# Inverse intermediate in contiguous weights, a second load of x, and a new order in a spectral filter and expert layer

## The chip, the core and the metric

The kernel runs on one core of a Trainium2 chip. The metric is the device time of one execution in microseconds (us), the median of three runs. Every instruction of the schedule is recorded first and issued later from one line, so the profile shows nearly all of them under line 552 (559 after the change), and they are told apart by the names of their tiles.

## What is computed

The input x has 2048 rows of 576 columns. It is normalised row by row, and two branches of the result are added to x. The reference, cut to what matters:

```python
xn = _layernorm(x, axis=-1)
# A: a filter in the two-dimensional spectrum
X = rfft2(xn)                      # 2048 x 289
y = irfft2(X * (w_r + 1j * w_i), (2048, 576))
# B: 32 heads, each picks one of 8 x 8 experts
q = einsum("nd,dhc->nhc", xn, w_q) # 32 heads, two halves of 128
s1, s2 = q1 . k1, q2 . k2          # 8 scores each
e = argmax(s1) * 8 + argmax(s2)
out = sum over heads of gelu(xn . u[e]) * v[e]
return x + y + out
```

The softmax over one candidate is 1.

## The kernel before

All Fourier transforms are matmuls with constant matrices. A row number is n = 16*n1 + t: n1 (128 values) lies on the partitions, t (16 values) counts tiles, so `XN` holds x as 16 tiles of 128 x 576. The stages, by the names in the program and the lines where they stand:

- `ln` (693), `folds` (733) and `dft128` (749), for each tile t: normalise, fold the 576 columns by symmetry to two parts of 289 (tiles `t`, `A`), and transform over n1 by matmuls. ScalarE or VectorE copies the results from PSUM (`banks`) to `AB`, four chunks of 128 partitions with 2048 columns, and `ABL`, the 66 rows left over. Columns are ordered in 16 groups of 128.
- `d_fwd` (990), two column groups at a time: the cosine and sine transform over the 576 columns. Its weights are 128 neighbouring columns of `AB` or `ABL` and its moving operand the constants `c` (145 columns). In fp32 each matmul is two weight loads and two matmul instructions in the profile. Result: `A2`, also named `A`.
- `s_fwd` (1016), four groups at a time with 32x32 weights `fw`, then `s_mul` (1032): the rest of the row transform, and the product with the filter `Wt` on VectorE (products into `y` and `t`, then two sums).
- `s_inv` (1044), two groups at a time: the first part of the inverse row transform. Its weights are columns of `y` (32 rows, tile position by row), its moving operand the 64 columns of `iv`. The 289 columns of `y` are covered by three chunks of 128 that start at 0, 161 and 49; the third is only there for the columns 128 to 160, and half of it is thrown away. The results are copied back over `AB` and `ABL`, to the same columns, one copy of 512 elements and two small ones for each group.
- `d_inv` (1067), for two tiles t and t+1: the inverse column transform, of the same shape as `d_fwd`. Row n of tile t stands in column 16*n + t of `AB`, so its weights are 128 columns that lie 16 elements (64 bytes) apart. Then ScalarE, VectorE and GpSimd unfold the result (`es` and `eo`, named `y` and `t` in the profile; the sum is named `A`).
- `fin` (1096), for each tile: the last 128-point transform and the experts' output are summed in PSUM, VectorE adds x from `XN` in place (`sc` is a scale), and SyncE stores the tile.
- The expert branch: `fold_part` (825) folds keys into `w_q` (32 loads `w` of 576 KB), `fold_scale`, `fold_end` and `fold_last` make the score weights `MU` and `MUL`; `x_t` (889) loads and scales x transposed (`xf`, `xT`); `scores` (905), `route` (932) and `combine` (954) compute, for two tiles, 448 scores and 64 expert activations, the maxima (`mx`), and the expert coefficients `CAT`. `wt`, `iv` and `id16` in these stages are small constants of their own.

The order is not that of the program. A planner (`_Plan`, 316) records every instruction with a modelled cost, groups matmuls, and then issues them by a list of priorities, `RANK` (142), under limits on PSUM tiles (`LIMIT`, 199). For work that several engines can do, `PICK` (133) holds one letter each: v VectorE, a ScalarE, g GpSimd. Each engine runs its instructions in order, and all DMAs are issued in order by SyncE.

Of the kernel before, what the change touches and what calls it, by code (L numbers as in the profile page):

```python
# [10 lines left out]
F32 = mybir.dt.float32  # L11
# [15 lines left out]
def _consts():  # L27
# [12 lines left out]
    k1 = np.arange(128) ^ np.arange(128) // 8 % 4 * 2  # L40
# [48 lines left out]
    iv = iv.reshape(8, 2, 128, 96).transpose(0, 2, 1, 3).astype(np.float32)  # L89
# [44 lines left out]
    "vgvgagvvvvaavggvgaavggvvaagggvaavgvvvaaavgvgvaavgvvavavvvgvavvggvvaavggvvvavvvvaavgvvvavagvvvgavgggv"  # L134
    "vavvvggaaaaagavggaggvvggavvgavggavavvgvggvggvaaaavvvvgvgavvagvaaavvvgagggavggagvaaavggvgvgggvaaaaaga"
    "gggavvgggvavvavvgavgggvggagaavaavgggggvgaavaavgaavgvavgggvavvvaavgavggavgggaavvavgggggggavvaaavvgvva"
    "aaaagvvvavagggggvgavggggagagvggvagagvgvgvvagggggagavvgvvagvvvgvgavagvgvg"
# [178 lines left out]
class _Plan:  # L316
# [9 lines left out]
    def cost(self, eng, m, out, ins, kw):  # L326
        n = 1
# [5 lines left out]
        if eng == "tensor":  # L333
# [3 lines left out]
            if kw.get("tile_position"):  # L337
                q = _parts(ins[0])
                return c * q[0] * q[1] / 16384, 230.0
# [873 lines left out]
```

## Time and profile before

| | |
|---|---|
| three runs | 253.95, 254.94, 255.24 us; median 254.94 |
| the profiled execution | 254.09 us, of which the span from the first to the last instruction is 252.3 |
| TensorE matmuls (PE) and weight loads (PEld) | 225.0 us busy (89%), 159.1 us (63%) |
| VectorE (DVE) | 195.0 us (77%) |
| ScalarE (ACT) | 76.2 us (30%) |
| GpSimd (POOL) | 107.7 us (43%) |
| moved by DMA | 41.75 MB, mean 165 GB/s |
| mean granted TensorE clock | 0.966 of full speed |

A row of a timeline gives the start, the length, the engine, the operation with output<-inputs, and in brackets the idle time before it with what ended it. A merged row's length reaches from the first start to the last end; TensorE's instructions overlap, so the distance of the starts tells the pace. A group's row gives the count, then the busy time, the mean ns of one, and the idle time just before.

### The profile page before, as it was taken

Reading aid. Unit: us, or ns where it says so; the run is one execution under the profiler, and the core shown is the slowest. Engines: PE = TensorE matmul, PEld = TensorE weight load, DVE = VectorE, ACT = ScalarE, POOL = GpSimd, SP = SyncE. Lnnn points to the kernel's source line nnn. Section 1 sums busy time; section 2 is a strip of 40 time slices with the busy share of each in tenths; the row PEclk is TensorE's granted clock in tenths of the full one; section 3 lists DMA queues with packets and bytes.
Section 4 is the critical chain, followed back from the end, with each engine's and each line's share of the span. In section 5 each row is a group of like instructions: output and inputs, shape, how many; then the busy total and the mean of one; then the engine's idle time right before and its main releaser. Section 6 shows DMA issues by size and latency. Waiting matters only on the chain.

```text
span 252.3 us, 6579 instructions
## 1 busy us (share of the span) xinstructions
PE 225.0 (89%) x2714; PEld 159.1 (63%) x2714; DVE 195.0 (77%) x458; ACT 76.2 (30%) x170; POOL 107.7 (43%) x155
## 2 busy tenths in 40 slices
PE   0335999999997898979999999989999999999994
PEld 0223756687466856875666444637788578888962
DVE  1979899946497168447977999998999897759574
ACT  2175853316304111372442320144220301110110
POOL 4557364523452006400650659364472464352330
PEclk9985899999999599999999999999999999999999
DMA  6999499999999649311231131013001111122116
GB/s 180 406 418 408 122 352 354 376 352 339 329 348 359 228 118 343 145 31 55 86 93 40 55 104 24 32 55 104 2 0 51 47 44 48 52 94 85 60 49 231
DMA packets 13998, 41.75 MB, mean 165 GB/s; under 512 B 1808, under 2 KB 4112, under 8 KB 13584
## 3 DMA queue, kind: packets, MB, share of 16 engines
q1 hardware_dynamic: 13968, 41.33, 46.3%
q8 instruction: 21, 0.34, 0.6%
q14 instruction: 9, 0.07, 0.1%
HBM read 36.61 MB, written 4.72 MB: 164 GB/s over the span
## 4 chain that ended last, share of the span: by engine, by line
PE 72%; DVE 15%; DMA 7%; issue 2%; ACT 1%; SPq 0%; POOL 0%; DVEq 0%; ACTq 0%
PE banks L552 72%; DMA w<-in_wq_dram 6%; DVE y L552 3%; DVE MT L552 2%; DVE w L552 2%; DVE t L552 2%; DMA c<-in_c_dram 2%; DVE A L552 1%; ACT AB L552 1%; DVE ABL L552 1%; DVE xT L552 1%; DVE mx L552 1%; DVE rr L552 0%; DVE xf L552 0%; SPq L552 0%
## 5 line engine op out<-in xcount | busy, mean ns | idle before, releaser
L552 PE MATMUL banks<-c,AB 128*128 128x145 f32 x256 | 50.1, 344 | 0.2 <-DVE ABL L552 0.2
L552 PEld LDWEIGHTS banks<-c,AB 128*128 128x128 f32 x256 | 46.8, 256 | 3.9 <-issue 1.4
L552 PE MATMUL banks<-MU,xT 128*128 128x512 f16 x192 | 45.9, 379 | 0.0
L552 PE MATMUL banks<-act,A 128*32 128x128 f32 (+1 forms) x256 | 27.5, 315 | 18.3 <-DVE act L552 10.5
L552 PEld LDWEIGHTS banks<-act,A 128*32 128x32 f32 (+1 forms) x256 | 21.4, 167 | 25.6 <-DVE act L552 10.5
L552 PEld LDWEIGHTS <-xT 128*128 128x128 f16 x224 | 20.8, 98 | 25.2 <-issue 1.9
L552 POOL TENSOR_TENSOR xT<-xf,xT 128x512 f16<-128x512 f32 (+1 forms) x23 | 20.4, 891 | 35.1 <-DVE xT L552 27.2
L552 POOL TENSOR_TENSOR y<-y,t 128x289 f32<-128x289 f32 x24 | 18.8, 810 | 30.0 <-DVE t L552 25.7
L552 POOL TENSOR_TENSOR A<-t 128x287 f32<-128x287 f32 (+3 forms) x32 | 23.1, 734 | 15.9 <-DVE t L552 7.3
L552 PEld LDWEIGHTS banks<-iv,y 32*128 32x128 f32 x768 | 23.6, 196 | 5.5 <-issue 2.5
L552 PE MATMUL banks<-iv,y 32*128 32x64 f32 x768 | 24.6, 282 | 2.6 <-issue 2.0
L552 PE MATMUL banks<-A,c 128*128 128x288 f32 x64 | 21.4, 416 | 0.0
L552 ACT ACTIVATE y<-banks 128x580 f32<-128x580 f32 x13 | 8.0, 651 | 42.0 <-PE banks L552 34.0
L552 ACT ACTIVATE AB<-banks 128x512 f32<-128x512 f32 x24 | 14.7, 616 | 18.8 <-PE banks L552 17.7
L552 PE MATMUL banks<-w,KP 128*32 128x288 f32 x256 | 20.2, 416 | 0.0
L552 POOL TENSOR_TENSOR t<-y 128x288 f32<-128x288 f32 x10 | 6.9, 692 | 22.0 <-ACT y L552 20.2
L552 POOL TENSOR_TENSOR t<-XN 128x289 f32<-128x289 f32 x15 | 12.5, 842 | 7.3 <-DVE A L552 3.1
L552 PE MATMUL banks<-c,ABL 32*128 32x145 f32 (+2 forms) x256 | 15.6, 357 | 0.0
L552 PE MATMUL banks<-A,fw 32*32 32x289 f32 x512 | 14.7, 413 | 0.2 <-ACT ABL L552 0.2
L552 DVE TENSOR_TENSOR A<-t 128x288 f32<-128x288 f32 (+3 forms) x32 | 14.6, 467 | 0.2
L552 DVE COPY ABL<-banks 64x128 f32<-64x128 f32 (+1 forms) x18 | 5.0, 288 | 12.2 <-ACT AB L552 9.0
L552 DVE SCALAR_TENSOR_TENSOR XN<-banks,sc,XN 128x576 f32<-128x576 f32 (+1 forms) x18 | 13.2, 746 | 1.3 <-PE banks L552 1.2
(130 smaller groups left out, 350.3 us busy)
## 6 DMA issues: line engine op xcount, KB each, us to landing
w<-in_wq_dram SPq DMA_DIRECT2D x32, 576.0 KB, 5.4
xf<-in_xT_dram SPq DMA_DIRECT2D x16, 320.0 KB, 3.0
Wt<-in_W_dram SPq DMA_DIRECT2D x8, 578.0 KB, 6.4
out_dram<-XN SPq DMA_DIRECT2D x14, 288.0 KB, 2.1
XN<-in_x_dram SPq DMA_DIRECT2D x3, 1154.0 KB, 10.2
XN<-in_x_dram SPq DMA_DIRECT2D x2, 577.0 KB, 5.2
iv<-in_iv_dram SPq DMA_DIRECT2D x8, 96.0 KB, 3.4
fw<-in_fw_dram SPq DMA_DIRECT2D x4, 192.0 KB, 6.2
```

Source lines behind the costliest of these rows:

```text
L552: fn(*[x.place() if isinstance(x, _Ps) else x for x in args], **{k: x.place() if isinstance(x, _Ps) else x for k, x in kw.items()})
```

## The change

1. `s_inv` writes to a new place and in a new layout. `XN` becomes a view of a larger tile `XI`, and after the folds are done the inverse intermediate lies in the same memory: for each tile t, four chunks of 128 neighbouring columns (`YT`) and one of the rest (`YLT`). `d_inv` takes these as weights. To make the layout one with matmuls that write 64 neighbouring columns, the constants `iv` are reordered: the moving operand is now 16 pieces of four elements, six apart. A copy from PSUM now writes single elements, 64 elements apart at the innermost step and 512 between tiles, and the copy of 512 elements is split in two of 256.
2. The third chunk of `s_inv` covers the 48 columns from 113 on, and its results take 48 partitions. In `d_inv` the leftover weights have 32 or 16 rows instead of 32.
3. x is overwritten by that, so `load_x` fetches it again, 16 loads of 288 KB into the memory of `AB`, which `d_fwd` has read by then. 14 tiles fit; the last two are loaded over the first two when these have been stored. `fin` adds from there.
4. The constants `wt`, `iv` (of the scores) and `id16` move into memory that the folds of `w_q` use, and so are written after these instead of early. The scratch of `ln` on ScalarE moves to a tile with six buffers. `iv` of `s_inv` has two buffers, not three.
5. The planner's cost of a matmul counts the weight load too, and `PICK` and `RANK` are new throughout.

```diff
-    k1 = np.arange(128) ^ np.arange(128) // 8 % 4 * 2
+    k1 = np.array([8 * g + 2 * (a ^ g % 4) + e for e in range(2) for a in range(4) for g in range(16)])
...
-    iv = iv.reshape(8, 2, 128, 96).transpose(0, 2, 1, 3).astype(np.float32)
+    iv = iv.reshape(16, 128, 3, 2, 16).transpose(0, 1, 4, 2, 3).reshape(8, 2, 128, 96).transpose(0, 2, 1, 3).astype(np.float32)
...
-    "vgvgagvvvvaavggvgaavggvvaagggvaavgvvvaaavgvgvaavgvvavavvvgvavvggvvaavggvvvavvvvaavgvvvavagvvvgavgggv"
+    "gggvavvvvaaavvvvavagvgggavggvvaaagvgvvvavgvvvvvvgggvavgvvvaaavgvgaaavvvgvaavgvvvaaggvgvavgvvgaaavvvg"
...
-    256, 294, 356, 417, 432, 525, 87, 484, 865, 888, 985, 269, 467, 374, 627, 757, 101, 541, 404, 387, 622,
+    239, 247, 252, 274, 291, 333, 222, 276, 218, 144, 412, 349, 225, 369, 299, 318, 473, 216, 99, 226, 109,
...
-    XN = K([128, 16, D + 1], F32, "XN")
+    XI = K([128, 10240], F32, "XI")
+    XN = XI[:, :9232].rearrange("p (t d) -> p t d", t=16)
+    YI = XI[:, :8192].rearrange("p (t c e k g) -> p c g k t e", t=16, c=2, e=4, k=4)
+    YL = XI[:, 8192:].rearrange("p (t e k g) -> p g k t e", t=16, e=2, k=4)
+    YT = XI[:, :8192].rearrange("p (t c n) -> p t c n", t=16, c=4)
+    YLT = XI[:, 8192:].rearrange("p (t n) -> p t n", t=16)
...
-                j, b = T([128, D], BF, "wa", 1, "t2"), rr[:, 3, t + i:t + i + 1]
+                j, b = T([128, D], BF, "wa", 6, "y"), rr[:, 3, t + i:t + i + 1]
...
-                        o = (0, 161, 49)[c]
-                        P.matmul(p[:, k, q, c, :], y[r, ri, o:o + 128], s[r, q, 32 * ri:32 * ri + 64],
+                        o, n = ((0, 128), (161, 128), (113, 48))[c]
+                        P.matmul(p[:n, k, q, c, :].rearrange("p (t e) -> p t e", e=4), y[r, ri, o:o + n],
+                                 s[r, q].rearrange("p (t e) -> p t e", e=6)[:, :, 2 * ri:2 * ri + 4],
                                  start=(ri == 0), stop=(ri == 1), tile_position=(32 * k, 0))
         for q in range(NQ):
-            pq = p[:, :, q]
-            FP.copy(ABg[:, :, g + q, :].rearrange("p c (k n) -> p c k n", k=4),
-                    pq[:, :, 0:2].rearrange("p k c (b n) -> p (c b) k n", b=2))
+            pq = p[:, :, q].rearrange("p k c (t e) -> p k c t e", e=4)
+            for c in range(2):
+                FP.copy(YI[:, c, g + q], pq[:, :, c])
             for b in range(2):
-                FP.copy(ABLg[64 * b:64 * b + 64, g + q, :].rearrange("p (k n) -> p k n", k=4),
-                        pq[64:128, :, 2, 32 * b:32 * b + 32])
+                FP.copy(YL[64 * b:64 * b + 48, g + q], pq[:48, :, 2, :, 2 * b:2 * b + 2])
...
-                    P.matmul(pv[b][:, c, q, :], ABt[:, 2 * (c ^ b) + b, :, t + q], ic[:, b, c ^ b, :], start=(q == 0), stop=False)
+                    P.matmul(pv[b][:, c, q, :], YT[:, t + q, 2 * (c ^ b) + b, :], ic[:, b, c ^ b, :], start=(q == 0), stop=False)
...
-                    r = slice(32 * i, 32 * i + 32)
-                    P.matmul(pv[b][:, c, q, :], ABLt[r, :, t + q], il[r, :], start=False, stop=(q == 1),
+                    r = slice(32 * i, 32 * i + 32 - i % 2 * 16)
+                    P.matmul(pv[b][:, c, q, :], YLT[r, t + q, :], il[r, :], start=False, stop=(q == 1),
                              tile_position=(32 * i, 0))
...
+    def load_x(t):
+        XR[t] = ABf[:, 576 * (t % 14):576 * (t % 14) + 576]
+        Q.dma_start(XR[t], xs[:, t, :D])
...
-        x = XN[:, t]
+        x = XR[t]
...
+    for t in range(14):
+        load_x(t)
     y = d_inv(0)
     for t in range(0, 16, 2):
         n = d_inv(t + 2) if t < 14 else None
         for q in range(2):
             fin(t + q, y[:, q])
+            if t + q < 2:
+                load_x(t + q + 14)
```

The new order shows in three places that the prediction uses.

On TensorE late in the program, before (`c_72,AB` and `c_72,ABL` are the large and small matmuls of `d_inv`, `A_93,c_68` the first of `fin`, `id_98,MT` transposes of coefficients, which read `banks<-MT` after the change):

```order
L552 MATMUL banks<-c_72,AB 128x145 x6
L552 LDWEIGHTS MT
L552 MATMUL banks<-id_98,MT 128x128
L552 LDWEIGHTS MT
L552 MATMUL banks<-id_98,MT 128x128
L552 MATMUL banks<-c_72,AB 128x145 x2
L552 MATMUL banks<-c_72,ABL 128x145 x8
L552 MATMUL banks<-A_93,c_68 128x288
```

And now:

```order
L559 MATMUL banks<-c_72,XI 128x145 x6
L559 LDWEIGHTS MT
L559 MATMUL banks<-MT 128x128
L559 LDWEIGHTS MT
L559 MATMUL banks<-MT 128x128
L559 MATMUL banks<-c_72,XI 128x145 x26
L559 MATMUL banks<-A_93,c_68 128x288
```

The weights of both kinds come from `XI` (x26 is the rest of one call of `d_inv` and a whole one behind it), and the matmuls stand between the same neighbours as before, the transposes and `fin`.

On VectorE, from the last copies of the score weights to the first maximum (`mx`), before:

```order
L552 SCALAR_TENSOR_TENSOR MU<-banks,sc,MU 128x4x112
L552 CAST xT<-xf 128x640
L552 SCALAR_TENSOR_TENSOR MUL<-banks,sc,MUL 64x336
L552 COPY A_93<-banks 128x2x2x145
L552 TENSOR_TENSOR xT<-xf,xT 128x512
L552 TENSOR_TENSOR y<-banks,Wt 128x578 x4
L552 TENSOR_TENSOR t_92<-banks,Wt 128x578 x4
L552 TENSOR_TENSOR y<-y,t_92 128x289 x2
L552 TENSOR_TENSOR xT<-xf,xT 128x512
L552 TENSOR_TENSOR xT<-xf,xT 64x128
L552 COPY A_93<-banks 128x2x2x145
L552 TENSOR_REDUCE mx<-banks 128x128
```

And now:

```order
L559 SCALAR_TENSOR_TENSOR MU<-banks,sc,MU 128x4x112
L559 COPY XI<-banks 48x4x32 x4
L559 COPY XI<-banks 128x4x16x4 x2
L559 TENSOR_SCALAR xf<-xf,bx 128x640
L559 COPY XI<-banks 48x4x32
L559 TENSOR_TENSOR xT<-xf,xT 64x128
L559 CAST xT<-xf 128x640
L559 TENSOR_REDUCE mx<-banks 128x128
L559 TENSOR_TENSOR t_92<-banks,Wt 128x578
```

Eight products of a group stood ahead of the maximum; now evacuations of `s_inv` (`XI<-banks`) stand there, and the four `t` products of a group follow the maximum.

On SyncE, from the middle of the weight loads to the last of them, before:

```order
L552 DMA w<-in_wq_dram 128x1152
L552 DMA fw<-in_fw_dram 128x384
L552 DMA Wt<-in_W_dram 128x1156 x2
L552 DMA w<-in_wq_dram 128x1152 x2
L552 DMA iv<-in_iv_dram 128x192
L552 DMA w<-in_wq_dram 128x1152 x2
L552 DMA iv<-in_iv_dram 128x192 x2
L552 DMA xf<-in_xT_dram 128x640 x2
L552 DMA w<-in_wq_dram 128x1152 x2
L552 DMA fw<-in_fw_dram 128x384
L552 DMA w<-in_wq_dram 128x1152
```

And now (`AB<-in_x` is the second load of x):

```order
L559 DMA w<-in_wq_dram 128x1152 x5
L559 DMA AB<-in_x_dram 128x576
L559 DMA xf<-in_xT_dram 128x640
L559 DMA AB<-in_x_dram 128x576
L559 DMA w<-in_wq_dram 128x1152 x3
L559 DMA Wt<-in_W_dram 128x1156 x2
L559 DMA w<-in_wq_dram 128x1152 x5
L559 DMA iv<-in_iv_dram 128x192
L559 DMA AB<-in_x_dram 128x576
L559 DMA Wt<-in_W_dram 128x1156
L559 DMA fw<-in_fw_dram 128x384
L559 DMA w<-in_wq_dram 128x1152 x3
```

Three of the second loads stand ahead of the last three weight loads; 13 come later.

More of the change, by code (lines that the diff above doesn't have):

```diff
@@ L133 @@
 PICK = (
-    "vgvgagvvvvaavggvgaavggvvaagggvaavgvvvaaavgvgvaavgvvavavvvgvavvggvvaavggvvvavvvvaavgvvvavagvvvgavgggv"
-    "vavvvggaaaaagavggaggvvggavvgavggavavvgvggvggvaaaavvvvgvgavvagvaaavvvgagggavggagvaaavggvgvgggvaaaaaga"
-    "gggavvgggvavvavvgavgggvggagaavaavgggggvgaavaavgaavgvavgggvavvvaavgavggavgggaavvavgggggggavvaaavvgvva"
-    "aaaagvvvavagggggvgavggggagagvggvagagvgvgvvagggggagavvgvvagvvvgvgavagvgvg"
+    "gggvavvvvaaavvvvavagvgggavggvvaaagvgvvvavgvvvvvvgggvavgvvvaaavgvgaaavvvgvaavgvvvaaggvgvavgvvgaaavvvg"
+    "aavgvvvvvvaavvgaavvgavvvvggvvagvvvvaggvgvvgvavvvaavvgaaggaavgavavavvvvvavvvggvvgggvaavavgggvvgvgaaav"
+    "vvvvvaagggaggvvaaavaaavavaagggaggvgaavaaggvggggvaaaaaaavvaaggaaggggavaaaaaaagaaggavgvvgaavaagggggggg"
+    "aaaavaaagavaavavavaaggvvvvavgvggavavgvvgagagvgggagagvvggagagggvgagaggvgvagavggggavvgvvgg"
 )
@@ L142 @@
 RANK = (
[55 rows of a table removed]
[58 rows of a table added]
 )
 LIMIT = {"x": 2, "a": 4, "b": 4, "q": 8, "c": 4, "s": 2, "f": 1, "m": 2}
-WORDS = {"st": 48, "t1": 578, "t2": 288, "A2": 580, "y": 580, "w": 1152, "Wt": 1156, "xf": 640, "xT": 576,
+WORDS = {"st": 48, "t1": 578, "A2": 580, "y": 580, "w": 1152, "Wt": 1156, "xf": 640, "xT": 576,
          "act": 128, "mx": 128, "fw": 384, "iv": 192}
 def _masks():
-    m = np.zeros((128, 99), np.float32)
+    m = np.zeros((128, 79), np.float32)
     code = 2.0 ** np.array([0, -6, -12, -18, -30, -36, -42, -48])
-    m[:, 20:27] = code[1:]
-    m[:, 27:35] = code
-    m[:, 35:99] = np.tile(2.0 ** np.array([-18, -12, -6, 0]), 16)
+    m[:, 0:7] = code[1:]
+    m[:, 7:15] = code
+    m[:, 15:79] = np.tile(2.0 ** np.array([-18, -12, -6, 0]), 16)
     return m
@@ L335, in cost @@
                 return max(n, 128) / 2.4 * (2 if ins[0].dtype == F32 else 1) + 4, 230.0
-            c = max(n, 64) / 2.4 + (2.5 if n > 256 else 5) if ins[0].dtype != F32 else max(n, 64) * 4 / 2.4 + 8
+            k = ins[0].shape[1]
+            if ins[0].dtype == F32:
+                c = 2 * max(n / 1.2 + 2, k * (1.7 if ins[0].ap[1][0] > 4 else 0.87))
+            else:
+                c = max(max(n, 64) / 2.4 + (2.5 if n > 256 else 5), 56 if k == 128 else k / 1.2)
             if kw.get("tile_position"):
                 q = _parts(ins[0])
-                return c * q[0] * q[1] / 16384, 230.0
+                c = max(c * q[0] * q[1] / 16384, 33.3 if ins[0].dtype == F32 else 16.6)
             return c, 230.0
@@ L618, in _body @@
     Q.dma_start(kT, a["kT"])
-    mk = K([128, 99], F32, "mk")
+    mk = K([128, 79], F32, "mk")
     Q.dma_start(mk, a["mk"])
-    cst = mk[:, 35:99]
+    cst = mk[:, 15:79]
     fm = K([128, 4], I32, "fm")
@@ L639, in _body @@
     ABL = K([128, S], F32, "ABL")
-    ABg = AB.rearrange("p c (g n) -> p c g n", g=16)
-    ABLg = ABL.rearrange("p (g n) -> p g n", g=16)
-    ABt = AB.rearrange("p c (n t) -> p c n t", t=16)
-    ABLt = ABL.rearrange("p (n t) -> p n t", t=16)
+    ABf = AB.rearrange("p c n -> p (c n)")
     MU = K([128, 2, 4, 512], F16, "MU")
@@ L983, in load_iv @@
     def load_iv(g):
-        IV[g] = T([128, 2, 96], F32, "iv", 3)
+        IV[g] = T([128, 2, 96], F32, "iv", 2)
         Q.dma_start(IV[g], a["iv"][g // 2])
@@ L1093, in d_inv @@
         return y
+    XR = {}
+    @staged
+    def load_x(t):
+        XR[t] = ABf[:, 576 * (t % 14):576 * (t % 14) + 576]
+        Q.dma_start(XR[t], xs[:, t, :D])
     @staged
@@ L1121, in _body @@
     plan.gate = gate
-    wt = K([128, 448], BF, "wt")
-    V.tensor_copy(wt.rearrange("p (e m) -> p e m", e=7), mk[:, 20:27].unsqueeze(2).to_broadcast([128, 7, 64]))
-    iv = K([128, 8, 32], BF, "iv")
-    V.tensor_copy(iv, mk[:, 27:35].unsqueeze(2).to_broadcast([128, 8, 32]))
-    id16 = K([128, 128], F16, "id16")
-    V.tensor_copy(id16, idn)
     plan.gate = set()
@@ L1139, in _body @@
                 fold_end(c)
+    wt = view(RM[:, 608:], [128, 448], BF)
+    V.tensor_copy(wt.rearrange("p (e m) -> p e m", e=7), mk[:, 0:7].unsqueeze(2).to_broadcast([128, 7, 64]))
+    iv = view(RM[:, 832:], [128, 8, 32], BF)
+    V.tensor_copy(iv, mk[:, 7:15].unsqueeze(2).to_broadcast([128, 8, 32]))
+    id16 = view(RM[:, 960:], [128, 128], F16)
+    V.tensor_copy(id16, idn)
     plan.gate = set(gate)
```

111 rows, old and new, of the table RANK are left out of this document.

## The prediction

> **What bounds the kernel now.** I read the page's 40 slices first, then the chain of work that ended last, then the engines' busy time by stretches. From the page, the span, the slices (tenths busy) of TensorE (PE) and VectorE (DVE), TensorE's granted clock, and what the DMA engines moved:
>
> ```profile
> span 252.3 us, 6579 instructions
> ...
> PE   0335999999997898979999999989999999999994
> ...
> DVE  1979899946497168447977999998999897759574
> ...
> PEclk9985899999999599999999999999999999999999
> ...
> GB/s 180 406 418 408 122 352 354 376 352 339 329 348 359 228 118 343 145 31 55 86 93 40 55 104 24 32 55 104 2 0 51 47 44 48 52 94 85 60 49 231
> ```
>
> A slice is 6.3 us. TensorE is at 9 in nearly every slice from the fifth on, and the DMA engines carry 329 to 376 GB/s from the sixth to the thirteenth, some 82 us, and little after 100. VectorE is at 8 or 9 over much of the second half, and mostly lower in the last seven slices. The end of the chain (start, us, what):
>
> ```profile
> 165.60 83.43 PE banks L552 x577
> 249.05 0.52 DVE XN L552
> ```
>
> So the last 83 us are TensorE's work end to end, without a wait. The first score matmul and the first maximum over scores on VectorE, from the timelines:
>
> ```profile
> 115.12 1.04 PE L552 MATMUL banks<-MU,xT 128*128 128x512 f16 x4
> ...
> 128.02 1.08 DVE L552 TENSOR_REDUCE mx<-banks 128x128 f32<-128x896 f32 x1
> ```
>
> Busy time by stretches cut there (PE, PEld, DVE, ACT, POOL, clock, DMA share, GB/s):
>
> ```profile
> 115.12:128.02 12.90, 12.90 (x216) 7.38 (x213) 11.03 (x17) 4.36 (x6) 5.76 (x8) 1.00 0.25 73
> 128.02:165.60 37.58, 36.51 (x515) 20.02 (x511) 33.87 (x73) 11.19 (x26) 18.54 (x25) 1.00 0.21 57
> 165.60:220.00 54.40, 54.40 (x400) 40.46 (x400) 48.63 (x105) 12.52 (x28) 27.27 (x36) 1.00 0.14 46
> 220.00:249.55 29.55, 29.01 (x179) 23.62 (x177) 21.82 (x47) 3.05 (x5) 9.96 (x13) 1.00 0.27 101
> ```
>
> From the first score on TensorE is never idle for more than about 1 us in a stretch, at full clock; VectorE is the runner-up: 33.87 of 37.58 us (90%) and 48.63 of 54.40 (89%), then 74%. ScalarE and the DMA engines have room. What shortens TensorE here shortens the kernel, until VectorE is level with it.
>
> **The change part by part.** The profiled execution took 254.09 us: 252.3 of span and 1.8 around it; the median of the three timed runs is 254.94, 0.3% more. I sum against 254.09.
>
> *Contiguous weights in the inverse column transform (d_inv).* Forward (d_fwd, contiguous weights) and inverse (weights 16 elements apart) are the same matmuls in shape. From TensorE's timeline, d_fwd's 16 large and 16 small instructions and the start of what follows, then d_inv's:
>
> ```profile
> 123.60 2.15 PE L552 MATMUL banks<-c,AB 128*128 128x145 f32 x16
> 125.67 0.78 PE L552 MATMUL banks<-c,ABL 17*128 17x145 f32 x16
> 126.38 0.61 PE L552 MATMUL banks<-MU,xT 128*128 128x512 f16 x2
> ...
> 205.32 3.56 PE L552 MATMUL banks<-c,AB 128*128 128x145 f32 x16
> 208.81 1.17 PE L552 MATMUL banks<-c,ABL 32*128 32x145 f32 x16
> 209.91 0.75 PE L552 MATMUL banks<-A,c 128*128 128x288 f32 x2
> ```
>
> By starts, a large one takes 2.07/16 = 0.129 us forward and 3.49/16 = 0.218 inverse; a small one 0.71/16 = 0.044 and 1.10/16 = 0.069. How many there are, and how long the weight loads are (inverse, from the groups of the stretch after 163 us; then forward, from that before 66 us):
>
> ```profile
> L552 PE MATMUL banks<-c,AB 128*128 128x145 f32 x128 | 29.6, 381 | 0.0
> L552 PEld LDWEIGHTS banks<-c,AB 128*128 128x128 f32 x128 | 28.8, 310 | 0.7
> ...
> L552 PE MATMUL banks<-c,ABL 32*128 32x145 f32 x128 | 9.3, 405 | 0.0
> ```
>
> ```profile
> L552 PEld LDWEIGHTS banks<-c,AB 128*128 128x128 f32 x48 | 6.3, 190 | 1.6 <-issue 1.4
> ```
>
> 128 large ones save 0.089 each, 11.4 us; 128 small ones 0.025 each, 3.1 us. All lie in the stretch where nothing but TensorE is on the chain. Sum 14.5 us. The loads behind it are 310 ns strided and 190 contiguous, so the step is what costs.
>
> The Trainium skill ("TensorE: Matmul & The Clock Gate", section LDWEIGHTS (loading the stationary operand)) has a load's time go by its columns alone, 128/1.2 = 107 ns as an estimate, with no word of the step: by that rule this term would be zero. The trace's 310 against 190 speaks against it.
>
> *The third chunk of the inverse row transform (s_inv) with 48 columns.* TensorE's timeline, a half group of the forward row transform (32x32 weights) and an s_inv:
>
> ```profile
> 146.09 1.60 PE L552 MATMUL banks<-A,fw 32*32 32x289 f32 x64
> ...
> 170.12 2.91 PE L552 MATMUL banks<-iv,y 32*128 32x64 f32 x96
> ```
>
> An s_inv instruction takes 2.91/96 = 30 ns; 32 of the 96 now load 48 columns for 128. The most that I grant is the other row's 1.60/64 = 25 ns: 8 x 32 x 5 ns = 1.3 us over the kernel, the least nothing. I take 0.7, half of it after the first score. Against it: the moving operand now lies in pieces of four elements, six apart. If that slowed s_inv as the step slowed d_inv (3.49/2.07, 1.69 times), it would cost 0.69 x 8 x 2.91 = 16 us. No row shows such an operand; I take nothing, since the pieces are contiguous, and keep the loss as a rival.
>
> *Evacuation of s_inv.* One copy of 512 elements becomes two of 256, and the small pair stays; all now write single elements that lie at least 256 bytes apart. The copies after 66 us (contiguous runs) and those of the first 66 us that write pairs 128 bytes apart (dft128):
>
> ```profile
> L552 ACT ACTIVATE AB<-banks 128x512 f32<-128x512 f32 x11 | 6.6, 597 | 7.6 <-PE banks L552 6.6 <-DVE ABL L552 0.9
> L552 ACT ACTIVATE ABL<-banks 64x128 f32<-64x128 f32 x19 | 4.9, 271 | 12.0 <-PE banks L552 5.6 <-DVE AB L552 5.3 <-DVE ABL L552 1.0
> ...
> L552 DVE COPY ABL<-banks 64x128 f32<-64x128 f32 x13 | 3.6, 293 | 11.9 <-ACT AB L552 9.0 <-PE banks L552 1.7 <-ACT ABL L552 1.2
> L552 DVE COPY AB<-banks 128x512 f32<-128x512 f32 x5 | 3.5, 691 | 1.8 <-ACT ABL L552 1.2 <-PE banks L552 0.6
> ```
>
> ```profile
> L552 ACT ACTIVATE AB<-banks 128x512 f32<-128x512 f32 x13 | 8.1, 632 | 11.2 <-PE banks L552 11.1
> ...
> L552 DVE COPY AB<-banks 128x512 f32<-128x512 f32 x3 | 2.0, 676 | 0.0
> ```
>
> Pairs cost what runs cost (632 and 676 against 597 and 691), so I price single elements the same. A copy of 256 lies a third of the way from 128 to 512: 0.43 us on VectorE, 0.38 on ScalarE. By the order VectorE has 10 of these and 14 small ones, 8.4 us where it had 5 and 13, 7.3; ScalarE 22 and 18, 13.2 where it had 11.7. ScalarE's room hides its part.
>
> *VectorE after the first maximum.* The order puts the four products of a group (the `t` products) behind the first maximum that stood ahead of it, and takes evacuations away (4 of 256 and 2 small ones stay behind it, where 2 of 512 and 6 small ones did). One product and one of the three constant casts that now come after the folds:
>
> ```profile
> L552 DVE TENSOR_TENSOR t<-banks,Wt 128x578 f32<-128x578 f32 x16 | 11.3, 752 | 3.2 <-PE banks L552 3.2
> ...
> L552 DVE CAST wt<-mk 128x448 bf16<-128x448 f32 x1 | 0.6, 600 | 0.0
> ```
>
> Four products are 2.8 us, the copies come to 2.3 us instead of 3.1: 104.3 us (33.87 + 48.63 + 21.82) become about 106; the other engine picks nearly cancel by count (32 sums on VectorE in d_inv and the folds together before and after). The casts, below 2 us together, stand among the score weights' copies. In return the first maximum comes right behind the first 28 score matmuls (at most 0.26 us each, 7.3), not 12.9 us after their start.
>
> *The second load of x.* 14 of 16 tiles are asked for long before their use, at a time of little DMA traffic, and cost nothing there. But three stand ahead of the last weight load in SyncE's queue, in the stretch of 329 to 376 GB/s. The weight loads, and SyncE's waits for TensorE:
>
> ```profile
> w<-in_wq_dram SPq DMA_DIRECT2D x32, 576.0 KB, 5.4
> ```
>
> ```profile
> SPq L552 <- PE banks L552: 63.0, 29, 7.9
> ```
>
> Three reloads of 288 KB at 339 GB/s are 2.6 us of transfer at most. c16, 725 KB, leaves the way of the last x, 2.1 us at that rate. I set the time of the first score unchanged at 115.1, with 5 us either way, for the order before it is new too.
>
> *Sum.* TensorE from the first score: 133.9 us (249.03 - 115.12) less 14.9 is 119.0, so it ends at 234.1; with the 3.3 us behind it the span is 237.4 and the time 239.2. VectorE: 106 us from 122.4 on; at its best rate so far, 90%, it ends at 240.2, span 242.9, time 244.7. Without a wait it would end before TensorE. Slices at 9 show that it can come close to full, so I take a value nearer to TensorE's: **241.0 us**.
>
> **The rivals.** *VectorE becomes the bound.* If it keeps the rate of the whole stretch before (104.3 of 121.5 us, 86%), 106 us end at 245.7, which gives 250.2. For it: maxima, products and sums wait on TensorE and ScalarE in turns. Against: its last stretch was at 74% only because TensorE was late. Chance 0.15, for 245 to 251.
>
> *The single-element writes are slow.* At d_inv's 1.69 times, VectorE's copies gain 69%: 1.6 us of those after the first maximum and about as much of those just ahead of it, 3.4 us in all, 244.4. The Trainium skill ("SBUF — State Buffer", section Specifications (TRN2)) speaks for this: lines of 16 bytes, and less than two hits on a line cost; pairs would be free and single elements not, and the trace agrees on the pairs. Chance 0.10.
>
> *The part before the scores shortens too.* TensorE's timeline there has a hole:
>
> ```profile
> 76.96 4.12 PE L552 MATMUL banks<-iv,y 32*128 32x64 f32 x137 [0.70 <-DVE A L552]
> 83.03 3.26 PE L552 MATMUL banks<-iv,y 32*128 32x64 f32 x55 [1.95 <-issue]
> 86.22 3.52 PE L552 MATMUL banks<-c,AB 128*128 128x145 f32 x16
> 89.67 0.78 PE L552 MATMUL banks<-c,ABL 17*128 17x145 f32 x16
> ```
>
> 1.95 us idle, then 55 instructions at 58 ns for 30 (1.5 us) and a d_fwd of 3.45 for 2.07 (1.4), with the clock down in that slice. An order without it starts the scores 4.9 us earlier: 236. Chance 0.12.
>
> *Nothing is gained:* loads that don't depend on the step, or an s_inv slowed by its new operand by those 16 us: 254. Chance 0.04.
>
> *Slower: the queue.* SyncE issues in order, and a reload must wait until d_fwd has read AB; behind it stand the weight loads. At the longest wait seen, 7.9 us, three reloads hold the last weights back by 23.7, with transfers 26: 254.1 - 13 + 26 = 267. It turns the gain into a loss from 13 us of holding on. Against it: the reloads stand where d_fwd's matmuls of the first groups are due anyway. Chance 0.06.
>
> **How the numbers follow.** The forecast itself, 238 to 244, keeps 0.53. The range 235 to 249 leaves out half of the early case's lower part, the top of VectorE's, and the two last rivals. A measurement of this kernel tells about 0.5% from no change, so faster is 0.53 + 0.15 + 0.10 + 0.12 = 0.90, same 0.04, slower 0.06.
>
> **What would show it.** Right: d_inv's 16 large instructions about 2.1 us apart, its loads near 190 ns; no long TensorE wait after the first score; VectorE over 90% busy from the first maximum on. VectorE as the bound shows as TensorE waiting for DVE between d_inv and the final matmuls, and in a chain that runs through DVE; slow writes as XI copies over 0.5 us; the queue as a first score well after 115 us with PE waiting for `w`. I am wrong if d_inv keeps 3.5 us per 16, or the first score moves by more than 5 us.

## The result, and the profile after

The changed kernel takes 245.59 us (median of four runs, 243.70 to 246.40) where the kernel before took 254.70 on the same chip: a ratio of 0.963 with a 95% interval of 0.957 to 0.970. The forecast of 241.0 was 4.6 us too low; the time lies inside its range. Ratios here and below leave out executions more than 1.5% longer than the fastest of the same kernel, such as the profiled ones of numbers 1, 4, 9 and 10; medians and ranges keep them, so a median can lie above its ratio times the kernel before.

The profiled execution took 243.7 us. From its page, the span, the slices (6.05 us each) of TensorE and VectorE, and TensorE's granted clock:

```profile
span 241.9 us, 6632 instructions
...
PE   0263799989999959998999989998899999999994
...
DVE  1959998985995565962699989987589999799794
...
PEclk9999999999999997999999999997699999999999
```

TensorE is as full as before, but the clock dips twice: in slice 16 (90.7 to 96.8 us) and in slices 28 and 29 (163 to 175 us). Both places come back below.

The steps of the prediction, one by one. The inverse column transform `d_inv`, from TensorE's timeline: its 32 instructions and the start of what follows. Then its groups:

```profile
184.45 2.85 PE L559 MATMUL banks<-c,XI 128*128 128x145 f32 x32
187.24 0.61 PE L559 MATMUL banks<-MUL,xT 128*128 128x512 f16 x2
```

```profile
L559 PE MATMUL banks<-c,XI 128*128 128x145 f32 x128 | 17.8, 288 | 0.6 <-ACT XI L559 0.6
L559 PEld LDWEIGHTS banks<-c,XI 128*128 128x128 f32 x128 | 16.7, 189 | 1.8 <-ACT XI L559 1.1
```

By starts the 32 take 2.79 us where they took 4.59 (209.91 - 205.32), and a weight load 189 ns where it took 310: over eight steps 14.4 us, and 14.5 were forecast. The first score and the first maximum, from the timelines:

```profile
114.34 2.75 PE L559 MATMUL banks<-MU,xT 128*128 128x512 f16 x12 [0.67 <-ACT XI L559]
...
120.99 1.08 DVE L559 TENSOR_REDUCE mx<-banks 128x128 f32<-128x896 f32 x1
```

The first score starts at 114.34 (forecast 115.1) and the first maximum 6.65 us later (forecast 7.3). So what is missing comes after that, by this reading: TensorE was to need 119.0 us from the first score on, and its last matmul ends at 238.65 (the windows below end there), after 124.3.

The copies of `s_inv`'s results into `XI`, and who waits for them (us in all, times, longest):

```profile
L559 ACT ACTIVATE XI<-banks 128x256 f32<-128x256 f32 x22 | 12.6, 621 | 13.0 <-DVE XI L559 11.0 <-PE banks L559 1.9
...
L559 ACT ACTIVATE XI<-banks 48x128 f32<-48x128 f32 x18 | 6.7, 384 | 3.6 <-DVE XI L559 2.9 <-PE banks L559 0.5
...
L559 DVE COPY XI<-banks 128x256 f32<-128x256 f32 x10 | 5.8, 594 | 6.6 <-ACT XI L559 6.0 <-PE banks L559 0.6
L559 DVE COPY XI<-banks 48x128 f32<-48x128 f32 x14 | 4.8, 365 | 6.9 <-ACT XI L559 3.8 <-PE banks L559 3.0
```

```profile
ACT XI L559 <- DVE XI L559: 14.0, 14, 2.9
...
DVE XI L559 <- ACT XI L559: 9.8, 12, 2.8
...
PEld banks L559 <- ACT XI L559: 5.0, 3, 2.7
...
PE banks L559 <- ACT XI L559: 4.2, 4, 2.1
```

The copies cost 621, 384, 594 and 365 ns; forecast were 380, 270, 430 and 290. And ScalarE's and VectorE's copies wait for each other, 26 times, 23.8 us: the eight copies of one `s_inv` (the expectations call it a group) stand in one row, though they write different elements. All of them read the same four PSUM banks. The Trainium skill ("PSUM — Partial Sum Buffer", section PSUM bank collisions raise a hardware error) says that the compiler back end adds a dependency between any two instructions on different engines that touch one bank and 32-partition quadrant, reads against reads too; the waits here are of that kind (number 7 below bears this out), and the kernel before had them as well (its rows in the prediction name them, 5.3 and 9.0 us). A row was some 2.4 us long then (2 x 0.64 + 4 x 0.28) and is 3.9 now (4 x 0.61 + 4 x 0.37).

What TensorE does meanwhile, from its timeline (in brackets the idle time before a row, and what ended it):

```profile
79.21 5.95 PE L559 MATMUL banks<-iv,y 32*128 32x64 f32 x192
86.03 1.60 PE L559 MATMUL banks<-A,fw 32*32 32x289 f32 x64 [0.86 <-DVE XI L559]
89.77 0.69 PE L559 MATMUL banks<-w,KP 128*32 128x288 f32 x8 [2.15 <-ACT XI L559]
...
174.37 1.01 PE L559 MATMUL banks<-c,XI 128*128 128x145 f32 x6 [0.61 <-ACT XI L559]
```

Behind two `s_inv`, together 5.95 us, the next matmuls stand for 0.86 and 2.15 us. At the last `s_inv` the chain of waits (start, us, what) goes through the last seven copies, ScalarE's and VectorE's in turn from 170.60 on, and `d_inv` starts right behind them. Its end:

```profile
173.08 0.61 DVE XI L559
173.69 0.02 issue
173.72 0.61 ACT XI L559
174.33 0.04 issue
174.37 24.32 PE banks L559 x194
```

### The profile page after: what moved, and what is told of

It is laid out like the page before. It is cut to its first block, busy times and chain, and to the rows that moved or that the text cites. A ratio compares the mean times of both kernels' runs of the same rounds, so it can differ in the third digit from the quotient of the medians.

```text
span 241.9 us, 6632 instructions
## 1 busy us (share of the span) xinstructions
PE 212.7 (88%) x2714; PEld 142.7 (59%) x2714; DVE 194.9 (81%) x465; ACT 87.1 (36%) x189; POOL 97.4 (40%) x145
## 4 chain that ended last, share of the span: by engine, by line
PE 67%; DVE 19%; ACT 7%; issue 2%; DMA 2%; POOL 1%; SPq 0%; DVEq 0%
PE banks L559 67%; ACT XI L559 5%; DVE t L559 3%; DVE XI L559 3%; DVE A L559 3%; DVE w L559 2%; DVE mx L559 2%; DMA XI<-in_x_dram 2%; DVE MT L559 2%; DVE st L559 2%; ACT y L559 1%; DVE y L559 1%; ACT act L559 1%; POOL A L559 1%; DVE rr L559 1%
## 5 line engine op out<-in xcount | busy, mean ns | idle before, releaser
L559 PE MATMUL banks<-act,A 128*128 128x128 f32 (+1 forms) x256 | 27.1, 316 | 16.6 <-ACT act L559 10.4
L559 POOL TENSOR_TENSOR xT<-xf,xT 64x128 f16<-64x128 f32 (+1 forms) x25 | 21.2, 850 | 40.5 <-ACT xT L559 29.9
L559 PEld LDWEIGHTS banks<-act,A 128*128 128x128 f32 (+1 forms) x256 | 21.3, 168 | 23.7 <-ACT act L559 10.4
L559 POOL TENSOR_TENSOR A<-t 128x289 f32<-128x289 f32 (+3 forms) x32 | 24.4, 776 | 19.1 <-DVE t L559 10.6
L559 PE MATMUL banks<-iv,y 32*128 32x64 f32 (+1 forms) x768 | 26.3, 270 | 1.4 <-DVE w L559 0.4
L559 PEld LDWEIGHTS banks<-iv,y 32*128 32x128 f32 (+1 forms) x768 | 22.9, 173 | 5.5 <-issue 1.2
L559 PE MATMUL banks<-c,XI 128*128 128x145 f32 (+2 forms) x256 | 23.4, 298 | 0.6 <-ACT XI L559 0.6
L559 PEld LDWEIGHTS banks<-c,XI 128*128 128x128 f32 (+2 forms) x256 | 21.2, 187 | 3.0 <-ACT XI L559 1.1
L559 PE MATMUL banks<-c,AB 128*128 128x145 f32 x128 | 18.4, 292 | 0.0
L559 PEld LDWEIGHTS banks<-c,AB 128*128 128x128 f32 x128 | 16.5, 190 | 2.0 <-issue 0.5
```

The costliest lines, as they stand in the source:

```text
L559: fn(*[x.place() if isinstance(x, _Ps) else x for x in args], **{k: x.place() if isinstance(x, _Ps) else x for k, x in kw.items()})
```

## The experiments

**Theory A:** the missing time is the row of copies, made longer by single elements and by the hand-overs between the two engines; TensorE waits for its end. **Theory B:** VectorE sets the end; the copies matter as its load. **Theory C:** neither; the new order around the last inverse and the clock there. Eleven kernels, all made from the changed one, and that one again (number 11); unless said otherwise every instruction keeps its place in the order. The code shows the main lines of each edit. Ratios are to the kernel before, on the same chip:

| kernel | median us | ratio (95% interval) |
|---|---|---|
| changed kernel | 245.59 | 0.963 (0.957 to 0.970) |
| the same, again | 244.79 | 0.963 (0.958 to 0.969) |
| 1 pairs | 238.26 | 0.937 (0.932 to 0.941) |
| 2 all copies on ScalarE | 241.45 | 0.951 (0.947 to 0.956) |
| 3 storage of before | 253.95 | 0.989 (0.982 to 0.995) |
| 4 pairs, large copies merged | 240.12 | 0.942 (0.937 to 0.947) |
| 5 pairs, all on ScalarE | 236.97 | 0.936 (0.930 to 0.943) |
| 6 as 2, VectorE kept as busy | 241.71 | 0.951 (0.945 to 0.958) |
| 7 pairs, copies cut by bank | 238.59 | 0.938 (0.931 to 0.946) |
| 8 pairs, second load left out | 237.05 | 0.934 (0.929 to 0.940) |
| 9 pairs, third chunk of 128 | 239.65 | 0.934 (0.927 to 0.942) |
| 10 pairs 8 bytes apart | 238.86 | 0.938 (0.932 to 0.945) |
| 12 pairs, merged, on ScalarE | 236.52 | 0.932 (0.926 to 0.938) |

The repetition stood beside numbers 9, 10 and 12 on one chip. 

> The changed kernel as it is, beside the three kernels below on one chip: 244 to 247 us, 0.96 of the kernel before. If it came out near 238, the gains of the other runs would be the chip's and not theirs.

 It came out as the first time.

**1. Pairs.** The two results that lie side by side in PSUM are stored side by side in `XI`; the last matrix gets its rows in that order.

```diff
...
-    YI = XI[:, :8192].rearrange("p (t c e k g) -> p c g k t e", t=16, c=2, e=4, k=4)
+    YI = XI[:, :8192].rearrange("p (t b c g k e) -> p c g k t b e", t=16, b=2, c=2, g=16, k=4)
...
```

The next pair stands 256 elements on, 1,024 bytes; the expectation has 512 bytes.

> The changed kernel, with the two members of a pair side by side in XI (8 bytes together, the next pair 512 bytes on) and the rows of the last matrix permuted to match; every instruction stays where it is. Theory A, the missing 4.6 us are the copies of the inverse's results into XI, which write single elements 256 bytes apart and stand one behind the other: the copies of 256 fall from 621 ns (ScalarE) and 594 ns (VectorE) to about 380 and 430, those of 48 rows from 384 and 365 to about 270 and 290, eight copies per group take 1.3 us less, and the time falls from 245.6 to 241 us (239.5 to 242.5). Theory B, VectorE sets the end: it sheds 10 x 0.16 + 14 x 0.07 = 2.6 us, so 243 us. Theory C, the order around the last inverse and the clock there, whatever the copies cost: within 1 us of 245.6.

The copies of the kernel with pairs:

```profile
L559 ACT ACTIVATE XI<-banks 128x256 f32<-128x256 f32 x22 | 8.0, 389 | 13.1 <-DVE XI L559 12.1 <-PE banks L559 0.8
L559 ACT ACTIVATE XI<-banks 48x128 f32<-48x128 f32 x18 | 4.8, 271 | 4.7 <-DVE XI L559 4.0 <-PE banks L559 0.6
L559 DVE COPY XI<-banks 128x256 f32<-128x256 f32 x10 | 4.1, 422 | 4.5 <-ACT XI L559 3.8 <-PE banks L559 0.6
L559 DVE COPY XI<-banks 48x128 f32<-48x128 f32 x14 | 3.9, 281 | 7.2 <-PE banks L559 5.1 <-ACT XI L559 2.0
```

They cost what the prediction had put down for single elements, within 10 ns. The ratio falls by 0.0265, 6.7 us of 254.5: more than theory A's 4.6 (the median lies below its range), and far more than the 2.6 that VectorE sheds (B). C falls.

**2. All copies on ScalarE**, single elements kept (`turn_to` records a copy on another engine in the same place).

```diff
...
                 FP.copy(YI[:, c, g + q], pq[:, :, c])
+                turn_to("a")
...
                 FP.copy(YL[64 * b:64 * b + 48, g + q], pq[:48, :, 2, :, 2 * b:2 * b + 2])
+                turn_to("a")
```

> The changed kernel with all 64 copies into XI on ScalarE, in the same places of the program; single elements are kept. Theory A, the row of copies of one group is the wait: it stays 4 x 0.62 + 4 x 0.38 = 4.0 us long, less the hand-overs between the two engines (about 0.1 us each), so 244 to 246 us. Theory B, VectorE sets the end: it sheds 10 x 0.594 + 14 x 0.365 = 10.9 us, so 237 to 240 us. Theory C: within 1 us of 245.6.

Its copies, and its stretch from the first score to the first `d_inv` (columns as in the prediction):

```profile
L559 ACT ACTIVATE XI<-banks 128x256 f32<-128x256 f32 x32 | 17.5, 631 | 6.5 <-PE banks L559 6.4
L559 ACT ACTIVATE XI<-banks 48x128 f32<-48x128 f32 x32 | 11.8, 394 | 1.3 <-PE banks L559 1.1
```

```profile
111.86:172.70 60.84, 57.17 (x824) 31.75 (x823) 49.10 (x97) 30.69 (x67) 29.57 (x35) 0.94 0.30 89
```

3 us less, between what A and B expected. The copies are as dear as before and no engine waits for the other. The first score comes 2.5 us earlier (111.86 for 114.34); from there to `d_inv` nothing is gained (60.8 us, and 60.0 in the changed kernel). So hand-overs had a price, against what A had put down, or VectorE's load had. TensorE's own waits for the copies don't tell: they sum to 5.2 us, as in the changed kernel (5.1). Number 6 decides.

**6. As 2, with VectorE kept as busy:** where it had a copy, it reduces a constant.

```diff
...
+        if op.flex[2] == "v":
+            op.calls.append((plan.of["v"].obj.tensor_reduce, (dum, c16[:, 0:n]), {"axis": AX, "op": OP.max}))
```

> The second run (single elements, all copies on ScalarE), and where VectorE had a copy it now reduces 440 or 226 elements of a constant tile in SBUF, about as long as the copy was (0.59 and 0.37 us), whose result nobody reads; the output is not touched by it. Theory A, what the second run removed were hand-overs between the engines, not VectorE's load: 241.5 us as there (240.5 to 242.5). Theory B, VectorE's load set the end: back to the changed kernel's 245.6 (244.5 to 246.5).

```profile
L559 DVE TENSOR_REDUCE dum<-c 128x1 f32<-128x440 f32 x10 | 6.1, 607 | 0.2
L559 DVE TENSOR_REDUCE dum<-c 128x1 f32<-128x226 f32 x14 | 5.4, 386 | 0.3
```

11.5 us of VectorE's time are back, and the ratio is that of number 2 (0.951 and 0.951). Theory B falls: what number 2 took away were the hand-overs, not VectorE's load (the reductions don't wait for TensorE as the copies did). What a hand-over costs shows in the first 16 copies, in number 2 all on ScalarE, then in the changed kernel (first and last row):

```profile
82.42 6.46 ACT L559 ACTIVATE XI<-banks 128x256 f32<-128x256 f32 x16 [2.30 <-PE banks L559]
...
82.39 0.60 DVE L559 COPY XI<-banks 128x256 f32<-128x256 f32 x1 [0.58 <-PE banks L559]
...
88.88 0.79 DVE L559 COPY XI<-banks 128x256 f32<-128x256 f32 x2 [0.66 <-ACT XI L559]
```

On ScalarE alone they take 6.46 us, though their lengths sum to 8.2 (8 of 631 and 8 of 394 ns): nine of them start some 0.2 us before the one ahead has ended. In the changed kernel none does so behind a hand-over, and the row takes 7.28 us, 0.8 more. The longest wait of 2.9 us is no such price: ScalarE waits there for the copy at 82.39, for which VectorE itself had waited for TensorE. Of the 2.5 us by which number 2's first score is earlier, 0.9 lie in the stretch of this row, and 1.4 in the next, where the clock is full (0.78 in the changed kernel, see below).

**3. The storage of before**, under the order, picks, second load and 48-column chunk of the change.

The moving operand of `s_inv` lies in whole columns again, too.

```diff
...
-    YT = XI[:, :8192].rearrange("p (t c n) -> p t c n", t=16, c=4)
+    YT = XI[:, :8192].rearrange("p (c n t) -> p t c n", t=16, c=4)
...
```

> The order, engine picks, second load and 48-column chunk of the changed kernel, with the storage of before: the copies write runs of 32 elements, and d_inv's weights are again read 16 elements apart. Every instruction stays where it is. Weights by address step: d_inv's 32 instructions take 4.6 us again where they take 2.8, 14.5 us over the eight steps, and the copies cost about 380 and 430 ns, so 14.5 us above the kernel with pairs: 253 to 258 us. Weights by columns alone: d_inv stays at 2.8 us, and the time is that of the kernel with pairs, about 241.

```profile
181.41 4.66 PE L559 MATMUL banks<-c,XI 128*128 128x145 f32 x32
186.00 0.60 PE L559 MATMUL banks<-MUL,xT 128*128 128x512 f16 x2
```

4.59 us again for the 32 instructions. Against pairs the ratio is 0.0517 higher, 13.2 us; by starts it is 8 x 1.8 = 14.4. The address step is what the contiguous weights remove; the Trainium skill's rule that a load goes by its columns alone ("TensorE: Matmul & The Clock Gate", section LDWEIGHTS (loading the stationary operand)) would have left this run at the time of number 1. Everything else of the change together is worth little: 1.2% by the ratio, 2.9 us (0.989, interval 0.982 to 0.995), and 0.5 us by the medians of all executions (253.95 and 254.46).

**4 and 12. Two large copies made one**, on the engines of the change and all on ScalarE; **5**, pairs with all copies on ScalarE.

```diff
...
             for c in range(2):
-                FP.copy(YI[:, c, g + q], pq[:, :, c])
+                h = slice(32 * c, 32 * c + 32)
+                FP.copy(YI[:, g + q, :, h], p[:, :, q, c].rearrange("p k (t e) -> p k t e", e=2))
+            whole(YI[:, g + q], p[:, :, q, 0:2].rearrange("p k c (t e) -> p k (c t) e", e=2))
...
```

`whole` puts one copy of 512 in the place of the first of the two and leaves the other's place empty.

> Pairs as in the first run, and the two copies of 256 of one group's half made into one of 512, with the two chunks outermost in XI. Theory A: a copy of 512 in pairs costs what it cost before, 0.60 on ScalarE and 0.69 on VectorE, instead of two at about 0.4, so the copies of a group take another 0.3 us less, of which about half is on the path: 239 to 241 us, at or below the first run. Theory B: VectorE sheds 2.6 us and some 0.1 us for each merged copy on it, 242 to 243. Theory C: within 1 us of 245.6.

> Pairs, as in the first run, and all 64 copies into XI on ScalarE, as in the second. Theory A, TensorE waits for the row of copies of a group, whose length is the copies plus the hand-overs between the engines (a copy on VectorE also waits in VectorE's own queue): both parts go, the row is 4 x 0.38 + 4 x 0.26 = 2.6 us, and the time falls below either run alone, 235 to 238 us. Theory A with hand-overs that cost nothing once the copies are short: 238 to 239, as with pairs alone. Theory B, VectorE's load: it sheds 10 x 0.43 + 14 x 0.29 = 8.3 us against pairs alone, 231 to 234 us.

> Pairs, all copies on ScalarE, and the two large copies of a half made one of 512: the row of a group falls from 4 x 0.38 + 4 x 0.27 = 2.6 us to 2 x 0.62 + 4 x 0.27 = 2.3 us. Theory A with room: TensorE waited no more than 0.9 us for these copies in the run with pairs on ScalarE, so nothing is left to win, 236 to 238 us. Without such room, the row being on the path still: 8 x 0.3 = 2.4 us less, 234 to 235 us.

All three have the ratio of pairs alone within the intervals (0.942, 0.936, 0.932 to 0.937): once the copies are short, hand-overs and a still shorter row are worth nothing that this can tell. The 8.3 us that number 5 takes from VectorE bring nothing either, where B expected 231 to 234. Number 12 has the lowest ratio of all, 3.3% under the changed kernel's (0.932 for 0.963). The stretches between the same six marks in the program (start of the second `s_inv` pair; the 8 `w` matmuls after it; three `MT` transposes; the first score; the first `d_inv`; the last matmul), first in the changed kernel, then in number 12:

```profile
79.21:89.77 10.56, 7.55 (x261) 6.19 (x257) 6.23 (x17) 3.70 (x8) 0.29 (x1) 1.00 0.86 329
89.77:97.66 7.89, 7.82 (x113) 3.39 (x114) 4.98 (x11) 0.00 (x0) 1.48 (x2) 0.78 0.68 228
97.66:114.34 16.68, 15.83 (x298) 12.72 (x298) 10.50 (x27) 10.31 (x22) 4.14 (x6) 1.00 0.76 242
114.34:174.37 60.03, 57.46 (x824) 32.68 (x823) 51.05 (x102) 26.85 (x57) 30.46 (x35) 0.94 0.31 90
174.37:238.65 64.28, 63.92 (x472) 45.31 (x472) 58.68 (x127) 14.08 (x29) 29.29 (x42) 1.00 0.22 77
```

```profile
80.23:88.41 8.18, 8.04 (x260) 6.14 (x256) 1.96 (x5) 5.04 (x15) 0.29 (x1) 1.00 1.00 382
88.41:94.86 6.45, 6.38 (x114) 3.02 (x114) 5.25 (x11) 0.00 (x0) 1.58 (x3) 1.00 0.82 290
94.86:111.21 16.35, 15.98 (x298) 12.60 (x298) 10.48 (x25) 9.22 (x21) 3.84 (x5) 1.00 0.81 258
111.21:166.45 55.24, 54.72 (x830) 30.88 (x824) 46.47 (x94) 25.05 (x58) 29.63 (x35) 1.00 0.33 98
166.45:230.73 64.28, 63.92 (x472) 45.21 (x472) 58.08 (x124) 13.99 (x29) 29.36 (x42) 1.00 0.22 77
```

Number 12 is shorter by 2.4 and 1.4 us in the first two stretches, by 0.3 in the third, by 4.8 between first score and `d_inv`, and by nothing after it; 8.9 in all, of which 1.0 was lost again ahead of the first mark. TensorE's waits for the copies fall from 5.1 us to 0.3. But not all of the 8.9 us are waits: 1.4 are clock in the second stretch, 0.78 for 1.00, and 2.7 in the fourth, 0.94 for 1.00 with PE busy 57.46 us for 54.72 on the same work. Without these 4.8 are left. What starts the dips stays open. The second trace of the changed kernel has them in the same stretches (0.74 and 0.97), but so has that of number 4, with short copies (0.70 and 0.94):

```profile
PEclk9995599999999976999999999997699999999999
```

And in number 5 the clock stood at 0.50 from 163 to 165 us, though TensorE's longest idle time since 150 was 0.17 us. So it isn't shown that the copies bring about the dips; the 6.7 us of number 1 are a difference of several executions of each kernel, with the dips that they had. In the last stretch VectorE is 90% busy (58.08 of 64.28) and TensorE has 63.92 of 64.28 all the same.

**7. Large copies cut by PSUM bank**, ScalarE on the first two, VectorE on the other two.

```diff
...
-                FP.copy(YI[:, c, g + q], pq[:, :, c])
+                k = slice(2 * c, 2 * c + 2)
+                FP.copy(YI[:, g + q, k], p[:, k, q, 0:2].rearrange("p k c (t e) -> p k (c t) e", e=2))
+                turn_to("av"[c])
...
```

> Pairs, and the four large copies of a group cut by PSUM banks: two read the first two banks, on ScalarE, two the other two, on VectorE; so the engines need not take turns for them. The small copies still read all four banks and take turns. VectorE has 16 large copies instead of 10. Theory A, the length of the row: where the large copies run side by side it is up to 0.8 us shorter per group, 236 to 238 us. Theory B, VectorE's load: six more copies of 0.43 us, 239 to 241 us. If turns cost nothing: 238.3, as with pairs alone.

```profile
ACT XI L559 <- DVE XI L559: 9.4, 10, 2.0
...
DVE XI L559 <- ACT XI L559: 5.6, 9, 1.3
```

```profile
81.88 1.21 ACT L559 ACTIVATE XI<-banks 128x256 f32<-128x256 f32 x3 [2.26 <-PE banks L559]
81.94 0.43 DVE L559 COPY XI<-banks 128x256 f32<-128x256 f32 x1 [0.60 <-PE banks L559]
```

Cut by bank, large copies of the two engines run at the same time, which those of the changed kernel never do; so it is the banks that they take turns for. 19 waits, 15.0 us, are left where number 1 has 24, 21.9 us: the small copies, which stand between the large ones, still read all four banks and take turns with everything. The ratio is that of pairs. With short copies the turns cost nothing that this can tell, though the waits of number 1 sum to nearly as much as the changed kernel's 23.8 us: that sum is no measure of what the turns cost. Whether a cut by bank would have helped the dear ones was not tried.

**8. Second load of x left out**, on top of pairs: each of its 16 loads brings one row of 128.

```diff
+        plan.ops[-1].calls = [(nc.sync.dma_start, (XR[t][0:1], xs[0:1, t, :D]), {})]
```

> Pairs, and the second load of x brings one row of 128 only, in the same 16 places of SyncE's queue; the last addition so adds what lies in AB for the other rows. Theory: the second load costs nothing, 238.3 us (237.5 to 239). Rival, its 4.7 MB hold up the weights and later loads: 235.5 to 237 us.

0.934 for 0.937: 0.7 us, inside the intervals; the median of 237.05 lies between the two ranges that were expected. That the second load costs nothing isn't contradicted; by the two intervals up to some 2.5 us can't be excluded.

**9. Third chunk of 128 columns again**, on top of pairs.

```diff
-                        o, n = ((0, 128), (161, 128), (113, 48))[c]
+                        o, n = ((0, 128), (161, 128), (113, 128))[c]
```

> Pairs, and the third chunk of the inverse takes 128 columns of weights again instead of 48 (256 instructions; the copies read the same 48 rows as before). By the traces, where 32 rows by 48 columns start about 30 ns apart and 32 rows by 128 columns too: no change, 238 us within 0.7. By the prediction's term: 0.7 us more, 239. By the weights' columns, if the load were what is waited for: 256 x 0.033 x 80/128 of four side by side, up to 1.3 us more, 239.6.

```profile
105.91 4.23 PE L559 MATMUL banks<-iv,y 32*128 32x64 f32 x141
110.39 1.77 PE L559 MATMUL banks<-iv,y 32*128 32x64 f32 x51 [0.25 <-issue]
```

141 instructions in 4.23 us are 30 ns each, as with 48 columns (5.95/192 = 31 in the changed kernel's row above), and the ratio does not rise (its interval alone would not tell 0.7 us). By the starts the term of 0.7 us is nothing.

**10. Pairs 8 bytes apart**, with a member of the next group's pair between them.

```diff
...
+    YI = XI[:, :8192].rearrange("p (t b c h k e l) -> p c h l k t b e", t=16, b=2, c=2, h=8, k=4, l=2)
...
```

> Pairs whose two members stand 8 bytes apart instead of 4, with a member of the next group's pair between them; everything else as with pairs. If a copy costs by the number of 16-byte pieces that it touches, one with two elements in each costs what neighbours cost: 0.38 (ScalarE) and 0.43 us (VectorE) for 256, and the time is that of pairs, 238 us. If it is neighbours that count, or single elements as such: 0.62 and 0.59 us, and the time is the changed kernel's, 245 us.

```profile
L559 ACT ACTIVATE XI<-banks 128x256 f32<-128x256 f32 x22 | 8.0, 389 | 13.1 <-DVE XI L559 12.3 <-PE banks L559 0.6
...
L559 DVE COPY XI<-banks 128x256 f32<-128x256 f32 x10 | 4.1, 422 | 4.9 <-ACT XI L559 4.2 <-PE banks L559 0.6
```

To the nanosecond the cost of neighbours. By these runs a copy is dear where each element lies 256 bytes or more from the one before, and cheap with two that lie 4 or 8 bytes apart; runs of 32, in number 3, cost no less (382 and 422 ns). Where between 8 and 256 bytes the limit lies, no run shows. The rule that the prediction cited from the Trainium skill ("SBUF — State Buffer", section Specifications (TRN2)), with two hits on a line of 16 bytes, agrees with these runs on both sides: one hit 621 and 594 ns, two 389 and 422.

## Why the prediction was right, and where not

- **Contiguous weights, 14.5 us on the path:** right in mechanism and size (14.4 by starts, 13.2 by ratios 3 and 1).
- **Evacuation of `s_inv`:** the step that failed. It said: "Pairs cost what runs cost, so I price single elements the same." The row of pairs was no row of single elements: 256 of these cost 232 ns (ScalarE) and 172 ns (VectorE) more than pairs. It also said "ScalarE's room hides its part". It had room by the sum, but the copies of both engines stand in one row and TensorE waits for its end, so length counted wherever it lay: 6.7 us by the ratios of 1 and the changed kernel. How much of that is TensorE's waits and how much the clock stays open. That the copies of the two engines wait for each other stood in the rows of before that the prediction quoted (9.0 us of VectorE's `ABL` copies behind ScalarE's `AB`), and was read past.
- **The rival "the single-element writes are slow",** given 0.10 and 244.4 us, is what happened, and its sign, copies into `XI` over 0.5 us, was there. Its place was wrong: it put the price into VectorE's load, which number 6 shows to be worth nothing. That its time came near is luck.
- **First score unchanged at 115.1:** 114.34, but by two errors that cancel. In number 12 it starts at 111.21: the new order does shorten the part before, as the rival with 0.12 had it, and the copies, with the clock's first dip, took most of that back.
- **TensorE needs 119.0 us from there:** 119.5 in number 12 (111.21 to 230.73, at full clock), 124.3 in the changed kernel.
- **VectorE between full and 90%, 1.8 us on top:** not needed. At 90% it held nothing up. By luck the term made up for 1.8 us of what the copies cost.
- **Sum of the profiled execution:** -0.8 at the first score, +5.3 after it, -1.8 for VectorE make the 2.7 us between 241.0 and its 243.7; the rest of the 4.6 is that this execution was the fastest of four.
- **48 columns, 0.7:** nothing (number 9). **Moving operand in pieces:** nothing, as taken. **Second load:** nothing that can be told (number 8).
- **A reading:** the stretch of 329 to 376 GB/s, which the prediction gives as "some 82 us", is eight slices, 50 us; it ends at 82.

## What to carry to other kernels

When a layout is changed for the reader's sake, price the writer by a row with as many neighbours written together, not by the nearest stride. Copies out of the same PSUM banks on two engines are one row; read its length, and who waits for its end, before calling an engine's room a cover. An unchanged mark, such as a first score at the forecast time, may be a gain and a loss that cancel.

## What the runs showed of the hardware

- Fp32 copies from PSUM to SBUF, 256 elements a partition: 621 (ScalarE) and 594 ns (VectorE) with each element 256 bytes or more from the one before; 389 and 422 in pairs, whether 4 or 8 bytes apart. For 128 elements on 48 partitions: 384 and 365 against 271 and 281.
- A matmul with 32 rows of fp32 weights starts every 30 ns or so, with 48 columns of weights as with 128, and with a moving operand of whole columns as with pieces of four.
- A load of 128 x 128 fp32 weights took 189 ns from neighbouring columns (changed kernel) and 311 from columns 64 bytes apart (number 3).
- TensorE's granted clock was 0.78 over 7.9 us of the changed kernel, behind waits of 0.86 and 2.15 us, and 1.00 through the same work of number 12 without them; in number 5 it was 0.50 for 2 us behind idle times of 0.17 us at most. What sets it off these runs don't show.
